# Moving a transformer block's later weight loads behind its first dense query copies, with a new prologue order

## The chip, the cores and the metric

One core of one Trainium2 chip. The metric is the device time of one execution in microseconds (us); lower is better. Times are medians of several runs, and runs of one kernel spread by 1 to 4 us, so differences of 1 us are read from repeated rounds or from the traces only.

## The reference, cut to what matters

```python
# x: 2048 tokens x 640; 32 query heads of 20, one key head, one value head; hidden size 1728; bf16
xn = layernorm(x)                                  # no scale, no shift
q, k, v = xn @ wq, xn @ wk, xn @ wv                # k and v are shared by all heads
p = softmax(q @ k.T / sqrt(20))                    # 32 heads x 2048 x 2048 scores
out = x + (p @ v) @ wo + silu(xn @ w1) @ w2
```

## The kernel before: the parts that matter here

The kernel is not written down instruction by instruction. A list scheduler with a small time model decides, while the program is built, which instruction each engine gets next; constants at the top of the file steer it. A changed constant or dependency can so reorder all engines. Where the model sees TensorE idle, the scheduler also gives it *filler products* with zeros, which add nothing to a result and are meant to keep its clock up; they count as busy in every view below.

The attention is done in *groups* of three (head, 512 queries) units, 43 groups in all, each in 16 *steps*, one for each tile of 128 keys: 688 steps. A step is three score products on TensorE (PE), and an exponential on ScalarE (ACT). Mostly ScalarE takes two of the three units (a tile 1024 wide) and VectorE (DVE) turns the third into an exponential by a clamp on integers; GpSimd (POOL) prepares what follows the clamp. In some steps ScalarE takes all three (1536 wide). The rule:

```python
    def want_dve(self, t):                     # may VectorE take the third unit of step t?
        if t < DVE_FROM or t % KT >= KT - NOD or t >= self.T - DVE_LAST:
            return False
        ...                                    # cut: how far VectorE's work reaches beyond TensorE's
        return back < DVE_TH
```

At the end of a group its result leaves PSUM through VectorE, is transposed by a DMA issued from SyncE's queue (SP), taken up by GpSimd, and its reciprocal is made on VectorE:

```python
        op = sc.dma("sp", lambda q: q.dma_start_transpose(self.UT[...], self.U[...]), [("U", up)], [("UT", up)], ...)
        ...                                    # four small GpSimd instructions
        sc.new("dve", 0.22, lambda v: v.reciprocal(rl, w[:, :, :, DH]), ...)
```

SyncE also issues nearly all loads, in order. In the kernel before, both fills of the query buffer, w1 and wo are given to it early, and w2 once the copy out of one of the last transposes is scheduled:

```python
        for par in range(2):
            ...                                # fill qT[:, :, par, :] with its constant rows
        load_w("sp", "1", ...)                 # w1, 5 pieces, 2160 KB
        load_w("sp", "o", ...)                 # wo, 5 pieces, 800 KB
...
                if n == max(i for i in range(13) if i not in DT):
                    load_w2()                  # w2, 14 pieces, 2160 KB
```

A *dense query tile* is a product with 128 rows of wq at once; its rows belong to several heads, so 7 small DMA copies carry it to its places before the scores of those heads can start. The *Newton steps* of the prediction are small instructions that make the reciprocal square roots of the normalization, for a batch of tiles of 128 tokens at once.

## Time and profile before

| kernel before | us |
|---|---|
| median of 3 runs (lowest, highest) | 739.36 (739.25, 740.0) |
| span of the profiled run | 738.2 |
| start of exponential 35, of exponential 40 | 70.3, 75.2 |
| from exponential 40 to the last, number 688 | 636.8 |
| from the start of the last exponential to the end (the tail) | 26.2 |

The table cuts the run where different things set the time. The start to exponential 40 is the prologue: loads, normalization, first products. The middle is the loop of exponentials. In the tail ScalarE has next to nothing to do, and TensorE works off what is left of the output products. The starts of single exponentials were counted in the trace.

Two more views than the prediction shows are needed. The first is VectorE's timeline at the eviction of group 0 (start, length, engine, line, operation):

```profile
53.95 0.68 DVE L972 CAST sbt<-psall 128x512 bf16<-128x512 f32 x1
```

The result was in SBUF at 54.6 us, so of the wait that the prediction calls hole C only 2 us were spent before the transpose's issue at 56.68, and 5.3 us after it. The second is TensorE's busy time, granted clock, DMA share and GB/s in stretches around that hole:

```profile
62.00:66.00 4.00, 1.22 (x21) 0.95 0.06 15
66.00:70.00 4.00, 3.67 (x25) 0.63 0.00 0
```

In the second stretch the clock is 0.63 of full speed: one stretch of 3.4 us, from 65.6 us, just as TensorE took up work again after its own idle time, was run at half clock.

### The profile page before, as it was taken

The numbers are of one execution on the slowest core, as the hardware profiler recorded it, in microseconds if no ns is written. First come the engines' busy times: TensorE is split into PE (matmuls) and PEld (weight loads), VectorE is DVE, ScalarE is ACT, GpSimd is POOL, SyncE is SP. The second block draws the span as 40 slices with busy tenths as digits, with TensorE's granted clock in tenths as the row PEclk, the third lists the DMA queues.
The fourth block names the chain that finished last, engine by engine and source line by source line (L and its number), as shares of the span: only waits on it lengthen the run. The fifth ranks groups of instructions, "written<-read, shape, count | busy, mean of one in ns | idle before, by whom it ended". The sixth has DMA issues, their size and how long they took to land.

```text
span 738.2 us, 18883 instructions
## 1 busy us (share of the span) xinstructions
PE 707.6 (96%) x6798; PEld 229.7 (31%) x6852; DVE 665.5 (90%) x1206; ACT 691.0 (94%) x780; POOL 538.4 (73%) x929
## 2 busy tenths in 40 slices
PE   9788999999999999999999999999999999999998
PEld 4422222233333223223333222222233332322235
DVE  7786998999999999989999999999999999989973
ACT  6886999999999999999999999999999999999940
POOL 5467777787787877777878877787788877777750
PEclk9999999999999999999999999999999999999999
DMA  6494010000003021100001101110002000200101
GB/s 191 80 338 108 20 25 17 21 17 16 9 16 44 17 58 40 32 10 9 9 8 27 33 16 40 54 32 16 8 9 44 10 8 16 80 9 8 31 16 36
DMA packets 58466, 29.14 MB, mean 39 GB/s; under 512 B 44390, under 2 KB 57734, under 8 KB 58374
## 3 DMA queue, kind: packets, MB, share of 16 engines
q1 hardware_dynamic: 56918, 27.71, 14.7%
q8 instruction: 56, 0.92, 0.5%
q10 hardware_dynamic: 1456, 0.22, 0.2%
q14 instruction: 36, 0.29, 0.1%
HBM read 11.36 MB, written 2.62 MB: 19 GB/s over the span
## 4 chain that ended last, share of the span: by engine, by line
PE 62%; ACT 17%; DVE 6%; issue 5%; POOL 1%; DMA 1%; DVEq 0%; ACTq 0%; POOLq 0%
PE psall L857 21%; PE psall L769 20%; ACT sbt L787 15%; PE psall L1146 9%; PE psall L1084 6%; DVE sbt L801 3%; PE psall L1151 2%; PE psall L1050 2%; ACT sbt L1092 1%; DVE sbt L869 1%; DMA sbt<-sbt 1%; DVE sbt L972 1%; PE psall L693 1%; POOL sbt L807 0%; DVE sbt L1057 0%
## 5 line engine op out<-in xcount | busy, mean ns | idle before, releaser
L787 ACT ACTIVATE sbt<-psall 128x1024 bf16<-128x1024 f32 (+2 forms) x688 | 657.8, 1091 | 16.8 <-PE psall L769 15.9
L807 POOL TENSOR_TENSOR sbt<-sbt 128x256 int32<-128x256 int32 x646 | 447.2, 698 | 149.3 <-DVE sbt L801 122.7
L801 DVE TENSOR_SCALAR sbt<-psall 128x512 int16<-128x512 f32 x646 | 432.5, 683 | 34.4 <-PE psall L769 26.4
L769 PE MATMUL psall<-sbt 32*128 32x512 bf16 x2048 | 269.1, 385 | 9.7 <-ACT sbt L787 4.7
L857 PE MATMUL psall<-sbt 128*32 128x512 bf16 x3524 | 270.2, 385 | 4.2 <-DVE sbt L869 2.0
L769 PEld LDWEIGHTS psall<-sbt 32*128 32x128 bf16 x2048 | 68.7, 91 | 252.8 <-issue 105.1
L869 DVE TENSOR_SCALAR sbt<-sbt 128x1536 int16<-128x1536 int16 (+2 forms) x230 | 134.8, 587 | 2.8
L857 PEld LDWEIGHTS psall<-sbt 128*32 128x32 bf16 x3524 | 67.8, 94 | 115.0 <-issue 75.4
L1146 PE MATMUL psall<-sbt 128*128 128x320 bf16 x448 | 86.2, 302 | 0.0
L1084 PE MATMUL psall<-sbt 128*128 128x512 bf16 (+1 forms) x242 | 75.7, 385 | 5.1 <-issue 3.7
L1146 PEld LDWEIGHTS psall<-sbt 128*128 128x128 bf16 x448 | 35.1, 97 | 43.4 <-issue 33.8
L1097 DVE SCALAR_TENSOR_TENSOR sbt<-sbt,psall 128x512 bf16<-128x512 bf16 (+1 forms) x56 | 38.1, 680 | 4.2 <-ACT sbt L1092 3.5
L1092 ACT ACTIVATE sbt<-psall 128x512 bf16<-128x512 f32 (+1 forms) x56 | 37.7, 674 | 0.0
L1084 PEld LDWEIGHTS psall<-sbt 128*128 128x128 bf16 (+1 forms) x280 | 18.8, 98 | 39.9 <-issue 29.6
L972 DVE CAST sbt<-psall 128x512 bf16<-128x512 f32 x43 | 29.3, 681 | 2.0 <-PE psall L857 1.9
L1151 PE MATMUL psall<-sbt 128*128 128x320 bf16 x144 | 28.7, 303 | 0.4 <-DVE sbt L1181 0.4
L1050 PE MATMUL psall<-sbt 128*128 128x512 bf16 (+1 forms) x81 | 26.6, 385 | 2.4 <-issue 1.4
L958 POOL TENSOR_TENSOR sbt<-sbt 128x240 bf16<-128x240 f32 (+2 forms) x44 | 25.7, 583 | 0.9 <-DMA sbt<-sbt 0.5
L944 POOL TENSOR_TENSOR sbt<-sbt 128x44 f32<-128x44 f32 x84 | 25.0, 298 | 1.0
L706 PE MATMUL psall<-sbt 128*128 128x512 bf16 (+2 forms) x67 | 17.5, 407 | 4.8 <-DVE sbt L1565 3.3
L942 POOL CAST sbt<-sbt 128x168 f32<-128x168 bf16 x42 | 14.2, 337 | 9.7 <-DMA sbt<-sbt 9.1
L1178 ACT ACTIVATE sbt<-psall 128x320 bf16<-128x320 f32 x4 | 1.5, 437 | 20.7 <-PE psall L1151 20.7
(94 smaller groups left out, 219.8 us busy)
## 6 DMA issues: line engine op xcount, KB each, us to landing
sbt<-in_A_x_dram SPq DMA_DIRECT2D x32, 160.0 KB, 3.6
out_dram<-sbt SPq DMA_DIRECT2D x15, 160.0 KB, 1.9
sbt<-in_B_w_dram SPq DMA_DIRECT2D x5, 432.0 KB, 7.4
sbt<-sbt SPq DMA_DIRECT2D x105, 20.0 KB
sbt<-in_B_w_dram SPq DMA_DIRECT2D x13, 160.0 KB, 5.8
sbt<-sbt SPq DMA_TRANSPOSE x68, 2.4
sbt<-sbt SPq DMA_DIRECT2D x1, 1024.0 KB, 7.3
sbt<-in_A_wo_dram SPq DMA_DIRECT2D x5, 160.0 KB, 6.8
```

What stands on the lines that cost most here:

```text
L769: ins = pe.matmul(self.bk(par3 + j), self.kT[r:r + SLOT, kk, kt * P:(kt + 1) * P], self.qT[r:r + SLOT, h // 4, (x // H) % 2, :], start=Tru ...
L787: return a.activation(self.E[:, b0 * QW:(b0 + na) * QW], self.ps[:, par3 * BANK:(par3 + na) * BANK], AF.Exp, scale=ACT_SCALE)
L801: return v.tensor_scalar(self.Z[:, zs, zp * QW:(zp + 1) * QW], self.bk(bb), 0.0, ZMAX, ALU.max, ALU.min)
L807: sc.new("pool", Y_TIME, lambda v: v.tensor_tensor(self.Y[:, zs, 1, zp * QW:(zp + 1) * QW].bitcast(I32), self.Z[:, zs, zp * QW:(zp + 1) * ...
L857: return pe.matmul(self.bk(UBANK, 0, QW, q * SLOT, (q + 1) * SLOT), self.v[:, w, kt, :], x, start=start, stop=stop, tile_position=(0, q * ...
L869: sc.new("dve", Y_SLOW + t_dve_4x(w), lambda v, k=k: v.tensor_scalar(self.Y[:, zs, k, 0:n * QW], Z, float(PH[k + 1][0]), None, ALU.add), z ...
L1050: return pe.matmul(self.bk(b, 0, QW, 0, rows), self.wq[:, k, lo:hi], self.xnT[:, k, c * QW:(c + 1) * QW], start=(k == 0), stop=(k == DC - 1))
L1084: return pe.matmul(self.bk(b, 0, QW, 0, rows), self.w1[:, k, fk * P:fk * P + rows], self.xnT[:, k, c * QW:(c + 1) * QW], start=(k == 0), s ...
L1092: sc.new("act", t_act(QW), lambda a: a.activation(t, src, AF.Tanh, scale=0.5), [("B", b)], [("tb", tp)], prio=X_PRIO, name=f"th{c}_{fk}")
L1097: sc.new("dve", t_dve_ps(QW), lambda v: v.scalar_tensor_tensor(out=self.hT[0:rows, fk, :], in0=t, scalar=1.0, in1=src, op0=ALU.add, op1=AL ...
L1146: return pe.matmul(self.bk(b, 0, 320), self.hT[0:rows, fk, i * P:(i + 1) * P], self.w2[0:rows, fk, e0:e0 + 320], start=(m == 0), stop=(m = ...
L1151: return pe.matmul(self.bk(b, 0, 320), self.oT[:, k, i * P:(i + 1) * P], self.wo[:, k, e0:e0 + 320], start=(m == 0 and src != "ps"), stop= ...
```

## The change

Its intent: give the first dense query tile's copies the queue before the bulk of w2, wo and the second fill, and search the prologue's order again with a scheduler that knows that GpSimd and VectorE hinder one another. Three settings of the loop go with it. The core of the diff:

```diff
+KT_ACT = (0,)                       # first step of each group: ScalarE takes all three units
-H_FIRST = 4
+H_FIRST = 8                         # hidden tiles ahead of the earlier chunk's output
-DVE_TH = 2.8
+DVE_TH = 3.4
-PV_HOLD = 9
+PV_HOLD = 11
-DT = (4, 5, 8, 9, 10, 11, 12, 13, 14, 15)
+DT = (4, 5, 6, 9, 10, 11, 12, 13, 14, 15)
-PRO = "t6 v0 k2 t7 k3 k4 q1 v1 v2 k5 k6 k7 v3 d0"
+PRO = "v0 t7 t8 v1 k2 k3 k4 q1 v2 d0 k5 k6 k7 v3"
-NW_ENG = ("dve", "pool", "dve", "pool")
+NW_ENG = ("dve", "dve", "dve")
-BATCHES = ((0, 4), (4, 8), (8, 12), (12, 16))
+BATCHES = ((0, 4), (4, 10), (10, 16))
 ... (cut: NORM_P, NORM_ENG, locks that keep VectorE and GpSimd apart in the model)
-        if t < DVE_FROM or ... or t >= self.T - DVE_LAST:
+        if t < DVE_FROM or ... or t >= self.T - DVE_LAST or t % KT in KT_ACT:
 ...
+            if c == 0 and m == 0:                       # first dense query tile: after its copies
+                self.late_loads(("qd", sl))
 ...
+        def late_loads(key):
+            load_w2([key])
+            load_w("sp", "o", ..., (), [key])           # wo
+            ...                                         # its scaling on GpSimd
+            qz(1, [key])                                # the second fill of the query buffer
```

More of the change, by code (lines that the diff above doesn't have):

```diff
@@ L75 @@
 UT_ISSUE = 1.05
-DT = (4, 5, 8, 9, 10, 11, 12, 13, 14, 15)
-NORM_P = 0.5
+DT = (4, 5, 6, 9, 10, 11, 12, 13, 14, 15)
+NORM_P = 4.5
 DVE_FROM = 8
-PRO = "t6 v0 k2 t7 k3 k4 q1 v1 v2 k5 k6 k7 v3 d0"
+PRO = "v0 t7 t8 v1 k2 k3 k4 q1 v2 d0 k5 k6 k7 v3"
 ACT_STATS = (4, 6, 9, 12, 14)
-NW_ENG = ("dve", "pool", "dve", "pool")
-NORM_ENG = ("pool", "pool", "pool", "pool", "dve", "act", "act", "dve", "act", "dve", "dve", "act")
-BATCHES = ((0, 4), (4, 8), (8, 12), (12, 16))
+NW_ENG = ("dve", "dve", "dve")
+NORM_ENG = ("pool", "pool", "pool", "pool", "act", "pool", "act", "act", "dve", "act", "act", "act")
+BATCHES = ((0, 4), (4, 10), (10, 16))
 class Op:
@@ L740, in want_dve @@
     def want_dve(self, t):
-        if t < DVE_FROM or t % KT >= KT - NOD or t >= self.T - DVE_LAST:
+        if t < DVE_FROM or t % KT >= KT - NOD or t >= self.T - DVE_LAST or t % KT in KT_ACT:
             return False
@@ L1302, in load_x, with load_w @@
             op.inc_no = 1
-        def load_w(eng, key, pieces, tag, nb, over=()):
-            deps = sc.deps_of((), [tag] + list(over))
+        def load_w(eng, key, pieces, tag, nb, over=(), extra=()):
+            deps = sc.deps_of(extra, [tag] + list(over))
             for f in pieces:
@@ L1327, in prologue, with load_w2 @@
                                                                self.B_w2[fk * P:fk * P + rows, :]))
-        def load_w2():
-            load_w("sp", "2", w2p, ("w2",), P * D * 2, [("xn", i) for i in range(14)] + [("idf",)])
+        def load_w2(extra):
+            load_w("sp", "2", w2p, ("w2",), P * D * 2, [("xn", i) for i in range(14)] + [("idf",)], extra)
         np_ = sc.new
@@ L1437, in norm @@
                 xa(n), self.xslot(n), self.rstd[:, n:n + 1], self.nb[:, n:n + 1], ALU.mult, ALU.add),
-                self.xkeys(n) + [("nb", n), ("rs", ra)], [("xn", n)], prio=prio, name=f"norm{n}")
+                self.xkeys(n) + [("nb", n), ("rs", ra)], [("xn", n)], prio=prio, name=f"norm{n}").lock = True
         def newton(a, b_, pr, eng):
@@ L1447, in nw @@
                 ch.append(np_(eng, 0.09 if eng == "dve" else 0.16, fn, r, w, prio=pr, name="nw"))
+                ch[-1].lock = True
                 if len(ch) > 1:
@@ L1496, in prologue, with qz @@
         tb = self.tb[:, 0, :]
-        for par in range(2):
+        def qz(par, extra=()):
             h0 = 2 if par == 0 else 0
             rep = bass.AP(self.tb, tb.offset, [list(tb.ap[0]), [0, HT - h0], list(tb.ap[1])])
-            op = sc.dma("sp", lambda q, par=par, h0=h0, rep=rep: q.dma_start(self.qT[:, h0:HT, par, :], rep), [("tb", 0)],
+            op = sc.dma("sp", lambda q: q.dma_start(self.qT[:, h0:HT, par, :], rep), [("tb", 0)] + list(extra),
                         [("qb", par, h) for h in range(4 * h0, H)], P * (HT - h0) * QW * 2, sem=sem(f"qz{par}"))
             op.inc_no = 1
+        qz(0)
         load_w("sp", "1", [lambda q, c=c: q.dma_start(self.w1[:, c, :], self.B_w1[c * P:(c + 1) * P, :])
                            for c in range(DC)], ("w1",), P * F * 2)
-        load_w("sp", "o", [lambda q, c=c: q.dma_start(self.wo[:, c, :], self.A_wo[c * P:(c + 1) * P, :])
-                           for c in range(DC)], ("wo",), P * D * 2)
+        def late_loads(key):
+            load_w2([key])
+            load_w("sp", "o", [lambda q, c=c: q.dma_start(self.wo[:, c, :], self.A_wo[c * P:(c + 1) * P, :])
+                               for c in range(DC)], ("wo",), P * D * 2, (), [key])
+            for c in range(DC):
+                pool(0.7, lambda g, c=c: g.tensor_scalar(self.wo[:, c, :], self.wo[:, c, :], 2.0, 1.0, ALU.mult, ALU.mult),
+                     [("wo",)], [("wo",)], prio=2.0)
+            qz(1, [key])
+        self.late_loads = late_loads
         def tr_job(n):
@@ L1523, in consume @@
                            prio=0.5 if n < 4 else 3.0, name=f"xT{n}")
-                if n == max(i for i in range(13) if i not in DT):
-                    load_w2()
             return Job(f"tr{n}", mms, xnk(n)[:1] + [("idb",)], consume)
@@ L1543, in consume @@
                                                                       ALU.mult), [("kT", j), ("offk",)],
-                       [("kT1", j)], prio=1.0, name=f"k1_{j}")
-                if j == KT // 2 - 1:
-                    for c in range(DC):
-                        pool(0.7, lambda g, c=c: g.tensor_scalar(self.wo[:, c, :], self.wo[:, c, :], 2.0, 1.0, ALU.mult,
-                                                                 ALU.mult), [("wo",)], [("wo",)], prio=2.0)
+                       [("kT1", j)], prio=1.0, name=f"k1_{j}").lock = True
             return Job(f"kv{j}", mms, [("xnT", 2 * j), ("xnT", 2 * j + 1), ("wk",), ("ost", 2, 0), ("ost", 2, 1)], consume)
```

## The prediction

> **What bounds the kernel now.** I read the page's busy shares first, then ACT's busy time in three stretches, then ACT's timeline through the prologue, then the other engines and the SP queue around its longest hole. Of the page, and of the stretches (busy us of ACT, clock, DMA share, GB/s):
>
> ```profile
> PE 707.6 (96%) x6798; PEld 229.7 (31%) x6852; DVE 665.5 (90%) x1206; ACT 691.0 (94%) x780; POOL 538.4 (73%) x929
> ...
> 20.00:80.00 60.00, 47.47 (x53) 0.94 0.58 166
> 80.00:700.00 620.00, 618.68 (x683) 1.00 0.10 24
> 700.00:738.20 38.20, 10.74 (x19) 1.00 0.10 27
> ```
>
> From 80 to 700 us ACT idles 1.3 us of 620: it works through the exponentials back to back, and nothing that only frees another engine can shorten this stretch. The 38 us at the end are other work (last products, output). Between 20 and 80 us ACT idles 60 - 47.5 = 12.5 us. A prologue change can win at most these, and pays for whatever it adds to ACT. ACT's timeline says where they are (start, length, count, idle before and its releaser):
>
> ```profile
> 23.13 1.73 ACT L1431 ACTIVATE sbt<-sbt 128x640 bf16<-128x640 bf16 x2 [0.99 <-DVE sbt L1468]
> ...
> 29.14 1.45 ACT L787 ACTIVATE sbt<-psall 128x1536 bf16<-128x1536 f32 x1 [2.53 <-PE psall L769]
> ...
> 40.55 1.94 ACT L787 ACTIVATE sbt<-psall 128x1024 bf16<-128x1024 f32 x2 [0.66 <-PE psall L769]
> 45.28 16.72 ACT L787 ACTIVATE sbt<-psall 128x1024 bf16<-128x1024 f32 x18 [2.80 <-PE psall L769]
> ...
> 67.94 1.94 ACT L787 ACTIVATE sbt<-psall 128x1024 bf16<-128x1024 f32 x2 [5.45 <-PE psall L769]
> ```
>
> Three holes: A (0.99 + 2.53 = 3.5 us) near 22 to 29 us, B (0.66 + 2.80 = 3.5 us) near 40 to 45, C (5.45 us) near 62.5 to 68; together 12.4.
>
> Hole A begins on VectorE, where nine tiny Newton steps on 128x4 values run beside GpSimd's four normalizations (18.38 to 21.84 us):
>
> ```profile
> 20.18 0.81 DVE L1457 TENSOR_TENSOR sbt<-sbt 128x4 f32<-128x4 f32 x1
> 21.03 0.82 DVE L1459 SCALAR_TENSOR_TENSOR sbt<-sbt 128x4 f32<-128x4 f32 x1
> ...
> 22.34 0.16 DVE L1457 TENSOR_TENSOR sbt<-sbt 128x4 f32<-128x4 f32 x1
> 22.54 0.16 DVE L1459 SCALAR_TENSOR_TENSOR sbt<-sbt 128x4 f32<-128x4 f32 x1
> ```
>
> The same step takes 0.82 us beside GpSimd and 0.16 us alone. Five slowed steps (0.53, 0.83, 0.81, 0.82, 0.42) cost 3.41 - 5 x 0.16 = 2.6 us. The copy out of the transpose of tile 6 waits behind them, and TensorE, in order, behind that copy.
>
> Hole B: step 14 needs the last key tile, whose product stands on TensorE behind 25 value products, after the last of ten transposes that SyncE issues from 19.29 to 37.4 us.
>
> Hole C starts in the SP queue (first two lines), shows on GpSimd (third) and then on VectorE (fourth):
>
> ```profile
> 49.09 7.55 SPq L1326 DMA_DIRECT2D sbt<-in_B_w_dram  x14
> 56.68 1.28 SPq L931 DMA_TRANSPOSE sbt<-sbt  x1
> ...
> 62.01 0.33 POOL L942 CAST sbt<-sbt 128x168 f32<-128x168 bf16 x1 [3.93 <-DMA sbt<-sbt]
> ...
> 64.27 0.23 DVE L949 RECIPROCAL sbt<-sbt 128x12 f32<-128x12 f32 x1 [3.73 <-POOL sbt L944]
> ```
>
> The transpose of group 0's result is issued at 56.68 behind the 14 loads of w2 and lands 5.3 us later; the median of the 42 such transposes is 2.4. GpSimd waits in order for it, VectorE for GpSimd, TensorE for VectorE, ACT for TensorE.
>
> **What the Trainium skill says.** "SBUF — State Buffer", the part on its two physically separate sides, says that VectorE in a two-port mode or with two SBUF inputs and GpSimd share one port pair as an exclusive lock: "the other fully blocks". The trace agrees: 0.82 against 0.16 us, and 0.82 is about one GpSimd normalization (0.88 us). "DMA: Bandwidth & Descriptors", Issuing engines are not separate DMA queues, says that all DMAs run on the same 16 engines and interleave; its Rules for kernel authors say to issue a DMA early and wait late. Hole C agrees: from 38 to 62 us the engines moved 334 GB/s at a DMA share of 1.02, and the small transpose waited. "Perfetto Trace Analysis", Identifying the Most-Contended Engine, takes occupancy as the measure for ScalarE but not matmul busy time for TensorE; so I follow ACT rather than PE's 96%.
>
> **The change part by part.** Counts come from the two instruction orders, durations from the rows of before.
>
> (1) The Newton batches become 4, 6 and 6 tiles, all on VectorE; 24 GpSimd steps of about 0.2 us go (4.8 us of an engine that is not the bound). The first six-tile batch comes ahead of GpSimd's normalizations, not beside them: most of the 2.6 us goes. That nothing overlaps is only the scheduler's model; no wait is added.
>
> (2) Six normalizations stand on ACT, against four. Two took 1.73 us, so + 2 x 0.87 = 1.7 us. Five stand in a row between exponentials 4 and 5, and need the statistics of all tiles. VectorE's order up to there, by its own rows: first batch from about 16.5 to 18.4 us; evictions and statistics 5.8 us, to 24.2; a copy 0.5; second batch 1.9, to about 26.5. Then 5 x 0.87 = 4.35 brings exponential 5 to about 30.9 us. Before, it came at 29.14, but with two more normalizations (1.7) still ahead of number 6: level, within an estimated 1 us. So hole A is filled with the moved work rather than won.
>
> (3) The last transpose should be issued about 35 us instead of 37.4, and the last key product stands ahead of step 11, before any value product. Hole B should nearly go: about -3 us.
>
> (4) Later loads: the queue becomes w1, four x tiles, three pieces of w2, the seven copies of the first dense q tile, eleven pieces of w2, wo, the 1024 KB fill of q, and only then the first result transpose (with two more behind it). What stands ahead of it is what stood before: w1 2160 + wo 800 + x 640 + w2 2160 + fills 1792 = 7552 KB, plus 128 KB of q copies. At the 334 GB/s of 38 to 62 us this is about 23 us, and the 5.4 us of copies may leave a gap of 1 or 2 us. From 35 us plus 2 to start, the transpose lands about 61 to 63 us; before it was 62.0. So I don't expect this part to relieve hole C by bandwidth. But the order is gentler: before, VectorE held the reciprocal behind its 23rd clamp (that of exponential 31), now behind its 24th (exponential 34, since the 33rd has none), and ACT arrives 3 us earlier. The chain from landing to the reciprocal was 62.01 to 64.27; from 62.6 it ends at about 65, and a clamp, a score and about 0.7 us later exponential 36 or 37 starts at about 66.4, where before number 33 started at 67.94: a gain of 1.5 + 3.5 x 0.93 = 4.8 us to this point, which holds (2), (3) and (4) together. If the transpose were in time, number 33 would start at about 59.5 (number 15 at 42.4, then 18 at 0.93 and one wide one): a gain of 8.4.
>
> (5) The first step of every group stays wholly on ACT (KT_ACT). Exponentials: 1536 wide 41 to 49, 1024 wide 632 to 625, 512 wide 15 to 14. By the busy time of the rows, 60.8/41 = 1.48, 597.4/632 = 0.945, 8.8/15 = 0.59: + 8 x 1.48 - 7 x 0.945 - 0.59 = + 4.7 us; where ACT runs back to back its starts are nearer 0.9 and 1.33 apart, so + 3.9. As ACT is the bound from 80 to 700 us, this lies on the path; about 0.9 of it falls before step 35, so + 3.0 to 3.8 remain. VectorE sheds 9 clamps of 0.67 us and about 5 us of their followers, about 11 us, which ACT's 1.3 us of idle cannot reward.
>
> (6) Eight h products before the earlier chunk's output: the same work, with one tanh (0.5 us) left for later. After the last scores 92 output products stand instead of 89: 3 x 0.13 = + 0.4 us.
>
> Sum: -4.8 + 3.4 + 0.5 + 0.4 = -0.5 if hole C stays in part; -8.4 + 4.3 = -4.1 if it goes.
>
> **Rivals.** *The late transpose remains the wait* (ahead: the same bytes in the same queue; against: it starts 2 us earlier, and consumers have more slack): 739.4 - 0.5, about 739. *The transpose comes in time*: -4.1, about 735; all holes gone, -12.4 + 4.7 + 1.7 + 0.4 = -5.6, about 734. *VectorE was the hidden pacer of the steady part* (90% busy; DVE releases many short TensorE waits), so its 11 us ease some of ACT's stretched exponentials: rows average 0.945 against 0.90 back to back, and if a tenth of that 632 x 0.04 = 25 us went, -2.5 more: about 731. *New conflict*: the second six-tile batch meets a GpSimd normalization, or five normalizations in a row starve the scores: +2 to +3, about 742.
>
> **Range and chances.** The change looks tuned for a gain, and my replay of orders is weakest in hole C, so I put the time between the first two rivals, nearer the second: 736.0 us, eight times in ten within 731 to 741. A gain over 2% is 14.8 us, more than all idle time of the prologue: 0.02. A loss over 2% would need a new stall of 15 us: 0.01. Within 2%: 0.97.
>
> **What would show it.** Right if: ACT's idle time between 20 and 80 us falls from 12.5 to some 4 to 6 us; no Newton step on VectorE takes 0.8 us; the 2.80 us wait near 45 us is gone; ACT stays 99% busy from 80 to 700 us; 49 wide exponentials are there. Hole C: the first result transpose lands at 61 to 63 us and GpSimd's wait for it stays above 3 us; if it lands before 59 us my queue argument is wrong and the time is nearer 733. If ACT shows idle time in the steady part, or the tail moves by over 1 us, the sum is wrong elsewhere.

## The result and the profile after

The changed kernel took 741.26 us (median of 4 runs, 741.11 to 744.0), the kernel before 739.31 on the same chip. The ratio is 1.0033, with a 95% interval of 1.0009 to 1.0057: the same at the 2% threshold, but slower, and 0.26 us above the predicted range of 731 to 741. Run again in a later batch the change gave 741.93 and 1.0026 (1.0012 to 1.0040): a small loss, not a gain.

The page's busy shares and ScalarE's stretches (busy us, clock, DMA share, GB/s) of the changed kernel:

```profile
PE 715.2 (97%) x6853; PEld 228.7 (31%) x6853; DVE 653.2 (88%) x1191; ACT 695.7 (94%) x782; POOL 526.4 (71%) x897
```

```profile
20.00:80.00 60.00, 50.74 (x54) 0.91 0.56 164
80.00:700.00 620.00, 619.17 (x683) 1.00 0.10 23
```

ScalarE's idle time in the prologue fell only from 12.5 to 9.3 us, and the middle is as full as before. The clock of the prologue fell from 0.94 to 0.91. (PE's 707.6 before against 715.2 is not 7.6 us more work: before, 54 matmul records are missing from the trace, 6798 against 6852 weight loads.)

ScalarE's timeline shows where the holes went (start, length, count, and in brackets the idle time before):

```profile
25.49 4.16 ACT L1434 ACTIVATE sbt<-sbt 128x640 bf16<-128x640 bf16 x5 [0.49 <-DVE sbt L1472]
29.56 7.26 ACT L788 ACTIVATE sbt<-psall 128x1536 bf16<-128x1536 f32 x6
37.08 1.02 ACT L788 ACTIVATE sbt<-psall 128x1024 bf16<-128x1024 f32 x1 [0.26 <-PE psall L770]
38.54 18.04 ACT L788 ACTIVATE sbt<-psall 128x1024 bf16<-128x1024 f32 x19 [0.44 <-PE psall L858]
...
68.32 1.94 ACT L788 ACTIVATE sbt<-psall 128x1024 bf16<-128x1024 f32 x2 [6.73 <-PE psall L770]
70.54 1.02 ACT L788 ACTIVATE sbt<-psall 128x1024 bf16<-128x1024 f32 x1 [0.29 <-PE psall L770]
71.99 1.02 ACT L788 ACTIVATE sbt<-psall 128x1024 bf16<-128x1024 f32 x1 [0.42 <-PE psall L770]
```

Holes A and B are gone: 0.49, 0.26 and 0.44 us stand where 3.5 and 3.5 stood. Hole C has grown from 5.45 to 6.73 us, and small waits follow it. Now the queue (SP), and the four engines that hand the wait on:

```profile
42.69 5.37 SPq L1067 DMA_DIRECT2D sbt<-sbt  x7
48.10 5.66 SPq L1329 DMA_DIRECT2D sbt<-in_B_w_dram  x11
53.80 2.48 SPq L1514 DMA_DIRECT2D sbt<-in_A_wo_dram  x5
56.32 0.69 SPq L1505 DMA_DIRECT2D sbt<-sbt  x1
57.06 12.59 SPq L932 DMA_TRANSPOSE sbt<-sbt  x2
```

```profile
48.66 0.68 DVE L973 CAST sbt<-psall 128x512 bf16<-128x512 f32 x1
63.79 0.33 POOL L943 CAST sbt<-sbt 128x168 f32<-128x168 bf16 x1 [7.56 <-DMA sbt<-sbt]
66.04 0.23 DVE L950 RECIPROCAL sbt<-sbt 128x12 f32<-128x12 f32 x1 [6.23 <-POOL sbt L945]
66.62 1.04 PE L858 MATMUL psall<-sbt 128*32 128x512 bf16 x8 [6.40 <-POOL sbt L808]
```

Group 0's result is in SBUF at 49.3 us, 5.3 us earlier than before. Its transpose stands in SyncE's queue for 7.7 us behind eleven pieces of w2, five of wo and a fill, is issued at 57.06, and GpSimd can take it only 6.7 us later, at 63.79; before, that was at 62.01. What the faster prologue won was spent in this queue, and 1.8 us more.

TensorE's busy time and clock after the hole:

```profile
62.00:66.00 4.00, 0.00 (x0) 0.60 0.28 22
66.00:70.00 4.00, 3.38 (x22) 0.50 0.09 22
70.00:74.00 4.00, 4.00 (x31) 0.62 0.05 11
```

TensorE was idle for 6.4 us (60.2 to 66.6) and then ran at half clock: the stretch lasts 10.2 us, from 62.8 to 73.0 us, three times the 3.4 us of before. Exponentials 36 to 40 start over 5.3 us, where the kernel before took 4.0. The Trainium skill, "TensorE: Matmul & The Clock Gate", Part 1: The HAM clock gate, says that an idle window of about 3.4 us halves TensorE's clock, that a busy window restores it, and that the window runs freely. The trace agrees on the length: the half-clock stretches last 3.4 and 10.2 us. It does not show a wholly idle window: in the 3.4 us before the fall at 62.8 us TensorE was busy for 0.8 us.

The account between the two profiled runs, by the cuts of the table:

| | before | after | difference |
|---|---|---|---|
| start of exponential 35 | 70.3 | 60.5 | -9.8 |
| exponential 35 to 40 | 4.9 | 13.1 | +8.2 |
| exponential 40 to 688 | 636.8 | 639.0 | +2.1 |
| tail | 26.2 | 26.9 | +0.8 |
| span | 738.2 | 739.5 | +1.3 |

Of the 9.8 us, 5.45 are hole C, which before lay ahead of number 33 and now lies ahead of number 36. Without it the prologue is 4.4 us faster. Hole C and the slow restart then take 8.2 instead of 5.45, and the loop and its tail take 2.9.

### The profile page after: what moved, and what is told of

It reads as the page before. It is cut to its first block, busy times and chain, and to the rows that moved or that the text cites. A ratio compares the mean times of both kernels' runs of the same rounds, so it can differ in the third digit from the quotient of the medians. Undisturbed runs are those within 1.5% of the kernel's fastest.

```text
span 739.5 us, 18880 instructions
## 1 busy us (share of the span) xinstructions
PE 715.2 (97%) x6853; PEld 228.7 (31%) x6853; DVE 653.2 (88%) x1191; ACT 695.7 (94%) x782; POOL 526.4 (71%) x897
## 4 chain that ended last, share of the span: by engine, by line
PE 71%; ACT 10%; DVE 5%; issue 4%; POOL 0%; DVEq 0%; ACTq 0%; POOLq 0%
PE psall L858 25%; PE psall L770 23%; PE psall L1149 10%; ACT sbt L788 8%; PE psall L1087 8%; DVE sbt L802 3%; PE psall L1051 2%; PE psall L1154 2%; ACT sbt L1095 2%; DVE sbt L1100 1%; DVE sbt L870 1%; PE psall L694 1%; DVE sbt L973 0%; PE psall L1217 0%; DVE sbt L1184 0%
## 5 line engine op out<-in xcount | busy, mean ns | idle before, releaser
L808 POOL TENSOR_TENSOR sbt<-sbt 128x256 int32<-128x256 int32 x637 | 438.9, 694 | 160.2 <-DVE sbt L802 140.3
L802 DVE TENSOR_SCALAR sbt<-psall 128x512 int16<-128x512 f32 x637 | 426.2, 685 | 47.6 <-PE psall L770 43.6
L770 PEld LDWEIGHTS psall<-sbt 32*128 32x128 bf16 x2048 | 69.1, 91 | 253.1 <-issue 76.5
L870 DVE TENSOR_SCALAR sbt<-sbt 128x1536 int16<-128x1536 int16 (+1 forms) x218 | 129.5, 596 | 2.2
L1087 PE MATMUL psall<-sbt 128*128 128x512 bf16 (+1 forms) x280 | 85.3, 384 | 2.8 <-DVE sbt L1100 2.6
L1149 PE MATMUL psall<-sbt 128*128 128x320 bf16 x448 | 84.0, 302 | 0.0
L1051 PE MATMUL psall<-sbt 128*128 128x512 bf16 (+1 forms) x95 | 28.7, 385 | 0.7 <-DVE sbt L1100 0.7
L1154 PE MATMUL psall<-sbt 128*128 128x320 bf16 x144 | 28.5, 303 | 0.3 <-DVE sbt L1184 0.3
L707 PE MATMUL psall<-sbt 128*128 128x512 bf16 (+1 forms) x74 | 18.7, 402 | 2.0 <-POOL sbt L1344 1.5
```

The costliest lines, as they stand in the source:

```text
L770: ins = pe.matmul(self.bk(par3 + j), self.kT[r:r + SLOT, kk, kt * P:(kt + 1) * P], self.qT[r:r + SLOT, h // 4, (x // H) % 2, :], start=Tru ...
L802: return v.tensor_scalar(self.Z[:, zs, zp * QW:(zp + 1) * QW], self.bk(bb), 0.0, ZMAX, ALU.max, ALU.min)
L808: sc.new("pool", Y_TIME, lambda v: v.tensor_tensor(self.Y[:, zs, 1, zp * QW:(zp + 1) * QW].bitcast(I32), self.Z[:, zs, zp * QW:(zp + 1) * ...
L870: sc.new("dve", Y_SLOW + t_dve_4x(w), lambda v, k=k: v.tensor_scalar(self.Y[:, zs, k, 0:n * QW], Z, float(PH[k + 1][0]), None, ALU.add), z ...
L1051: return pe.matmul(self.bk(b, 0, QW, 0, rows), self.wq[:, k, lo:hi], self.xnT[:, k, c * QW:(c + 1) * QW], start=(k == 0), stop=(k == DC - 1))
L1087: return pe.matmul(self.bk(b, 0, QW, 0, rows), self.w1[:, k, fk * P:fk * P + rows], self.xnT[:, k, c * QW:(c + 1) * QW], start=(k == 0), s ...
```

## The experiments

The theory: (i) the place of the first result transposes in SyncE's queue decides what the prologue's gain is worth; (ii) the hole costs more than its length, because TensorE restarts at half clock; (iii) the settings of the loop cost about 3 us. Rivals: the result transpose is not what the group waits for; moved work is only paid back later; the loop's settings pay for themselves. In what follows, e35 and e40 are the starts of exponentials 35 and 40; all from each run's one profile.

| run | median us | ratio to before (95%) | e35 | e40 | e40 to 688 | tail | span |
|---|---|---|---|---|---|---|---|
| before | 739.9 | 1 | 70.3 | 75.2 | 636.8 | 26.2 | 738.2 |
| the change (first profile) | 741.3 | 1.0033 (1.0009, 1.0057) | 60.5 | 73.6 | 639.0 | 26.9 | 739.5 |
| after_again | 741.9 | 1.0026 (1.0012, 1.0040) | 61.0 | 74.6 | 638.8 | 26.9 | 740.3 |
| tr_first | 736.0 | 0.9957 (0.9940, 0.9975) | 61.5 | 66.2 | 641.2 | 26.9 | 734.3 |
| split_late_2 | 735.7 | 0.9945 (0.9927, 0.9964) | 60.3 | 64.9 | 640.5 | 26.9 | 732.4 |
| before_w2_late | 737.3 | 0.9965 (0.9950, 0.9979) | 68.0 | 72.6 | 637.0 | 26.2 | 735.8 |
| loads_back | 747.3 | 1.0100 (1.0081, 1.0119) | 82.8 | 87.4 | 640.2 | 18.0 | 745.5 |
| steady_after | 741.9 | 1.0021 (1.0004, 1.0038) | 71.1 | 76.5 | 640.5 | 22.8 | 739.9 |
| steady_before | 747.2 | 1.0088 (1.0072, 1.0104) | 61.3 | 73.6 | 636.6 | 35.5 | 745.7 |

(The median of before is that of the later batches, 739.9 to 740.0; its profile is the first one. Each figure is rounded by itself, so a row's sum can be 0.1 off its span. The other runs' figures stand in their sections.)

### tr_first: the first result transpose ahead of the late loads

```diff
+            if g == 0:                                  # in end_group, after the transpose is given
+                self.late_loads(("U", 0))
-            if c == 0 and m == 0:                       # in the dense query tile
-                self.late_loads(("qd", sl))
```

> The changed kernel, with w2, wo and the second q fill queued only behind the first result transpose instead of ahead of it. My theory (the late transpose is the whole of hole C, with the half TensorE clock that follows it): the transpose lands within 3 us of its issue (6.7 before), GpSimd's wait for it falls from 7.6 to under 1.5 us, ACT's idle time between 20 and 80 us from 9.2 to about 2 us, the clock stays at 1.00 there, and the time falls by 7 to 9 us, to about 733. Rival (the loss is the work moved onto ACT): the hole goes but another in-order wait takes its place, time 739 or more.

Correct; 735.97 us, 0.9957 of the kernel before. Its queue, GpSimd's two pick-ups, and ScalarE's one new wait:

```profile
50.39 1.24 SPq L932 DMA_TRANSPOSE sbt<-sbt  x1
...
63.04 2.19 SPq L932 DMA_TRANSPOSE sbt<-sbt  x1
```

```profile
54.50 0.32 POOL L943 CAST sbt<-sbt 128x168 f32<-128x168 bf16 x1
...
68.73 0.32 POOL L943 CAST sbt<-sbt 128x168 f32<-128x168 bf16 x1 [1.92 <-DMA sbt<-sbt]
```

```profile
76.87 2.37 ACT L788 ACTIVATE sbt<-psall 128x1536 bf16<-128x1536 f32 x2 [1.82 <-PE psall L770]
```

The transpose was issued as soon as the result was in SBUF (49.69 + 0.68), hole C vanished, no half clock showed before the end, and e40 came 7.4 us earlier than in the changed kernel. The second transpose was issued 0.3 us after its result (62.06 + 0.68 us), but behind the moved loads it was picked up only 5.7 us later, and ScalarE's wait of 1.8 us followed. Theory (i) holds: this one place is worth 5 to 6 us of the change's time, where 7 to 9 were expected. The loop after e40 was 2.2 us longer than in the change, so some of the gain is given back.

### fill_hole: keep TensorE's clock through the hole

```diff
+        # behind the scores of step 34: 26 products with zeros, into the open bank, adding nothing
+        for _ in range(26):
+            pe.matmul(self.bk(UBANK, 0, QW, 0, 32), self.zero[:, 0:32], self.zero[:, 0:QW], start=False, stop=False, ...)
```

> The changed kernel with 26 extra products of zero weights (about 5.5 us) set on TensorE just ahead of the value product that waits in hole C; results are not altered. They end before that wait ends, so only the clock can change. If the half clock after the hole costs time: granted clock 1.00 between 62 and 74 us, exponentials 37 to 40 without their waits of 0.3 to 0.6 us, time lower by about 2 us, 739.3. If the clock plays no part: the time stays at 741.3.

Correct; 742.77 us, ratio 1.0035 (1.0022 to 1.0048): no gain in the whole. TensorE's busy time and clock over the hole:

```profile
62.00:66.00 4.00, 4.00 (x21) 1.00 0.76 95
66.00:70.00 4.00, 3.29 (x27) 1.00 0.00 0
```

The clock stayed at 1.00. From the end of group 0's reciprocal to exponential 36 it took 1.4 us instead of 2.05, and exponentials 36 to 40 took 3.6 us (69.45 to 73.08) instead of 5.3. So the half clock's local price is 2.3 us, 0.6 before exponential 36 and 1.7 after it; this part of theory (ii) is shown. In the total it was not seen. In the profiled run exponential 1 started 1.0 us later than in the change's, a half-clock stretch fell at 34.1 us and another at 279.9, exponential 35 started at 62.5, 2.0 us late, before the edit can have acted, and the loop after e40 took 640.9 us, 1.9 more than in the change. The timed runs' mean clocks are 0.995 in two and 0.997 to 0.998 in four, against 0.991 to 0.993 in the change; yet these four took 740.8 to 743.0 us, where the change took 741.1 to 744.0. Why the total did not gain stays open.

### no_kt_act: the rule on the first step taken out alone

```diff
-KT_ACT = (0,)
+KT_ACT = ()
```

> The changed kernel without the rule that keeps each group's first step on ACT (KT_ACT empty). My theory (ACT paces the steady part, so the extra width is paid in full): wide exponentials fall from 49 to about 40, the time falls by 3 to 4 us, to about 737.5; hole C is as it was. Rival (the rule relieves VectorE at each group's start and pays for itself): 741 or more, with more ACT idle time after 80 us.

748.99 us, 1.0117 (1.0103 to 1.0132), and the result was wrong (relative error 0.408); why was not found, so only its times are used, and with care. Only 10 exponentials are 1536 wide, against 49, where about 40 were expected; with the threshold at 2.8, in steady_before below, 39 are; that threshold and H_FIRST are all that differs. VectorE's busy time rose to 684.9 us. ScalarE idled 9.0 us between 80 and 700 us (0.8 in the change), as the rival said. It reached its last exponential at 699.2 us, 13.5 us before the changed kernel's, and the end came 8.5 us later. TensorE's busy time in the tail, first of this run, then of the changed kernel:

```profile
699.20:748.10 48.90, 43.62 (x287) 1.00 0.19 52
```

```profile
712.60:739.50 26.90, 23.55 (x177) 0.98 0.08 26
```

TensorE is 97% busy in the changed kernel (93% without the 24.0 us in which only filler products ran). Work taken from ScalarE does not shorten the run when TensorE does not get through its own earlier; the difference comes back as output products after the last exponential. My expectation that the rule's price lies in full on the path fell in this form.

### h_first_4: four hidden tiles first

```diff
-H_FIRST = 8
+H_FIRST = 4
```

> The changed kernel with four h products before the earlier chunk's output, as before the change. My theory: this part is worth only the tail: 89 or 90 output products after the last scores instead of 92, time lower by 0 to 1 us. Rival (the job order matters in the steady part): a change of over 2 us either way, seen as ACT idle time between 80 and 700 us.

Correct; 743.40 us, 1.0056 (1.0040 to 1.0072). The tail was 28.0 us, not shorter than the 26.9 of the change: the setting is not what lengthened it. By the ratios the run took about 2 us longer than the change (the intervals overlap), where 0 to 1 less was expected. This expectation was wrong.

### split_late: the loads in two steps, first try

The late loads are split: w2 after the first result transpose; wo, its scaling and the second fill after the second.

```diff
+            if g < 2:                                   # in end_group; the call in the dense tile goes
+                self.late_loads(("U", g))
 ...
+            if key == ("U", 0):
+                load_w2([key])
+                return
             load_w("sp", "o", ...)                      # then the scaling and qz(1, [key])
```

> The changed kernel with its late loads in two steps: w2 is given to SyncE once the first result transpose is, wo with its scaling and the second fill of the query buffer only once the second result transpose is. In tr_first the first transpose was issued at 50.4 us and cost ScalarE nothing, but the second stood behind w2, wo and the fill and made a wait of 1.8 us at 76.9 us. Theory (the place of the transposes in SyncE's order is what the prologue's gain hangs on): that wait goes too, ScalarE is idle no more than 2 us between 20 and 80 us outside the first group, no half clock between 60 and 80 us, 734.0 us against 736.0 of tr_first. Rival (the second transpose waits for something else, such as its own group's end, or wo arriving later holds up the first output projection): the same 736, or a new wait later.

735.32 us, 0.9927, but the result was wrong (relative error 0.93). The one difference from the mended run below is that the fill comes later too, so that is where the fault came in; a likely reason, not tested, is that the tile which the fill copies had been used again by then. Its times are left out of the argument.

### split_late_2: the same, with the fill back where it was correct

```diff
-            if c == 0 and m == 0:
-                self.late_loads(("qd", sl))
+            if g < 2:                                   # in end_group
+                self.late_loads(("U", g))
 ...
+            if key == ("U", 0):
+                load_w2([key])
+                qz(1, [key])
+                return
             load_w("sp", "o", ...)                      # after the second transpose, with the scaling
```

> As split_late, mended: w2 and the second fill of the query buffer go to SyncE after the first result transpose (where tr_first has them and was correct), wo and its scaling after the second. Theory: correct, the second transpose is issued within 1 us of its group's eviction, ScalarE waits for no scores between 60 and 110 us, and the time is that of split_late, 734.5 to 735.5 us, so at or a little under the 736.0 of tr_first and 6 below the changed kernel. Rival (what was gained in split_late hung on the wrong data or on the fill's place): 736 or more.

Correct; 735.68 us, 0.9945 of the kernel before. Its queue at the two transposes:

```profile
49.16 1.29 SPq L932 DMA_TRANSPOSE sbt<-sbt  x1
...
61.51 1.21 SPq L932 DMA_TRANSPOSE sbt<-sbt  x1
```

Both are issued as their results come (the evictions ended at 49.13 and 61.48 us), and ScalarE's longest wait between 20 and 110 us is 0.5 us, after which 31 instructions follow without a gap:

```profile
38.43 29.38 ACT L788 ACTIVATE sbt<-psall 128x1024 bf16<-128x1024 f32 x31 [0.50 <-PE psall L858]
```

It is busy 58.88 us of the 60 between 20 and 80. The time is 0.2 us above the range that was expected. It is the fastest correct version found, and it beats both kernels. Against tr_first (0.9957) the intervals overlap, so the second step's own worth, 1.3 us at e40, is not shown in the total.

### before_tr_first and before_w2_late: the same idea in the kernel before

In before_tr_first, w2, wo and the second fill go behind the first result transpose in the kernel before.

```diff
-                if n == max(i for i in range(13) if i not in DT):
-                    load_w2()
 ...                                                    # wo and the second fill leave their early places too
+            if g == 0:                                  # in end_group
+                self.late_loads(("U", 0))
```

> The kernel before with one thing changed: w2, wo with its scaling and the second fill go behind the first result transpose, nothing else of the change. Theory (hole C is one hole of 5.45 us in the kernel before, owed to the transpose's place alone): about 734.5 us, 5 less than before, and the holes A and B stay as they were. Rival (the hole is set by the group's own work on TensorE and VectorE, or later work fills up what is won): within 2 us of before.

Correct; 759.18 us, 1.0251 (1.0230 to 1.0271), so the expectation was off by 25 us. The transpose was issued at 56.73 us and GpSimd did not wait for it; but in this kernel the dense query tile's copies come *after* that transpose. The moved loads took their place in the queue (w2 at 58.34, wo at 65.05, the fill at 68.28, the copies at 69.06 us), ScalarE waited 10.3 us in one piece, and e40 came at 89.6:

```profile
69.06 6.59 SPq L1068 DMA_DIRECT2D sbt<-sbt  x7
```

```profile
74.31 0.60 ACT L1094 ACTIVATE sbt<-psall 128x512 bf16<-128x512 f32 x1 [10.29 <-DMA sbt<-sbt]
```

So both the copies and the transposes have to stand ahead of the bulk loads. In before_w2_late, w2 alone is moved, behind the second transpose:

```diff
+            if g == 1:                                  # in end_group
+                self.late_w2(("U", 1))                  # w2's 14 pieces
-                if n == max(i for i in range(13) if i not in DT):
-                    load_w2()
```

> The kernel before with w2's fourteen loads alone moved behind the second result transpose, so that the first transpose and the copies of the dense query tile go first; wo and both fills stay. In the kernel before the first group's result left the bank at 54.6 us, the transpose was issued at 56.7 and GpSimd went on at 62.0. Theory (the loads cost the transpose 2 us of issue and about 1.5 us of landing): issued at 54.7, GpSimd at about 58, the hole of 5.45 us down to about 2, and 736 us, 3.5 less than before. Rival (before_tr_first's 759 shows that the kernel before does not bear its loads moved at all): 739.5 or more.

Correct; 737.34 us, 0.9965 (0.9950 to 0.9979), 2.5 us less than before, where 3.5 was expected. The transpose and GpSimd's pick-up:

```profile
56.47 1.23 SPq L931 DMA_TRANSPOSE sbt<-sbt  x1
```

```profile
59.81 0.32 POOL L942 CAST sbt<-sbt 128x168 f32<-128x168 bf16 x1
```

GpSimd took the result 3.3 us after issue, without a wait, where it was 5.3 us behind w2's loads, and the hole of 5.45 us became one of 1.54:

```profile
65.72 1.94 ACT L787 ACTIVATE sbt<-psall 128x1024 bf16<-128x1024 f32 x2 [1.54 <-PE psall L769]
```

The exponentials themselves began 1.5 us later in this run and the clock was halved at 48.2 us; e40 gained 2.6. Fourteen loads put in another place gained 2.5 us, where the whole change lost 1.9.

### loads_back: the changed kernel with its loads where they were

```diff
         qz(0)
+        qz(1)
 ...                                         # wo early, w2 at the copy out of the last transposes; no late_loads
```

> The changed kernel with its loads where the kernel before has them (both fills and wo early, w2 behind the transposes of the normalized rows), all else of the change stays. Theory (in the changed kernel the late loads keep the first transpose from 49.3 to 57.1 us on SyncE and then lengthen its landing to 6.7 us): the loads are issued some 5 us earlier, but the copies of the dense query tile wait behind w2, so what the transpose wins the scores lose: ScalarE's idle time of 9.3 us from 20 to 80 us stays between 7 and 13 us, and 741 us, within 2 of the changed kernel. Rival (the late loads are the whole of the loss): 737 or less.

Correct; 747.30 us, 1.0100 (1.0081 to 1.0119). I had expected the two orders to be level. Its queue:

```profile
47.13 7.70 SPq L1327 DMA_DIRECT2D sbt<-in_B_w_dram  x14
54.94 5.42 SPq L1067 DMA_DIRECT2D sbt<-sbt  x7
60.40 10.21 SPq L932 DMA_TRANSPOSE sbt<-sbt  x2
```

The copies went out 12.2 us later than in the changed kernel (54.94 against 42.69), the transpose 3.3 us later, ScalarE was idle for 20.9 us between 20 and 80 us, where 7 to 13 were expected, and e40 came 13.7 us later, at 87.4; the shorter tail gave 8.9 us of that back. So the move that gives the change its name is good by itself: under the new prologue it is worth 5.4 us of the time. It was put in the right place for the copies, and the wrong one for the transposes. This transpose, behind the small copies instead of bulk loads, was picked up 2.4 us after its issue (GpSimd at 62.80), against 6.7.

### steady_after and steady_before: the loop's settings alone

KT_ACT, DVE_TH and H_FIRST of the change put into the kernel before (steady_after), and those of before put into the change (steady_before, shown here; steady_after is the reverse).

```diff
-KT_ACT = (0,)
+KT_ACT = ()
-H_FIRST = 8
+H_FIRST = 4
-DVE_TH = 3.4
+DVE_TH = 2.8
```

> The kernel before with the three steady settings of the changed kernel alone: the rule on the first key tile, the threshold at 3.4, eight hidden tiles first; its prologue and its loads stay. Theory (these settings cost 2.9 us between exponential 40 and the end): 742 us, 2 to 3 more than before. Rival (they cost nothing by themselves, as a search that chose them would suggest): within 1 us of 739.5.

> The changed kernel with the three steady settings of the kernel before: no rule on the first key tile of a head, the VectorE threshold at 2.8 instead of 3.4, four hidden tiles first instead of eight; its prologue and its late loads stay. Theory (the change's prologue wins about 1.6 us up to exponential 40 and its steady settings lose about 2.9 from there to the end): 738 us, 2 to 3 less than the changed kernel, with the stretch from exponential 40 to the end near the 663.0 us of the kernel before. Rival (the loss comes from the order that the prologue leaves behind, not from the settings): 741, as the changed kernel.

Both correct. Steady_after: 741.91 us, 1.0021 (1.0004 to 1.0038): a loss of about 1.5 us, less than expected. The loop took 3.7 us longer and the tail 3.3 less. Steady_before: 747.18 us, 1.0088 (1.0072 to 1.0104), where 738 was expected: the loop fell back to 636.6 us as expected, but the tail rose to 35.5. So neither "these settings cost 2.9 us" nor "they are harmless" is right for both prologues. What ScalarE saves in the loop, TensorE returns in the tail, by an amount that depends on the order that the scheduler finds. Why it returned 8.5 us for 2.4 in steady_before is shown in part only. TensorE's idle time there, summed over its records, is 24.4 us, and 24.3 in the change. But the time in which it ran nothing but filler products is 27.3 us against 24.0 (131 such products against 114), and the time with other products 693.9 against 691.3. So over half of the 6.1 us between the two spans went into filler, which the order decides; no run without filler was made, and the rest stays open.

### after_again: the change beside the last three

> The changed kernel itself, beside the three of this batch on the same chip. All theories expect the ratio of 1.0033 against the kernel before again, within its interval (1.0009 to 1.0057), a half clock episode somewhere between 60 and 75 us, and ScalarE idle about 9 us between 20 and 80 us.

Correct; 741.93 us, 1.0026, as before. The half-clock stretch was there again (10.2 us, from 63.5), ScalarE was idle 9.8 us between 20 and 80 us, and the first result transpose was issued at 57.92 and picked up at 64.95 us.

## Why the prediction was wrong, by its own steps

**Bounds and holes: right, with one omission.** ScalarE is over 99% busy in the middle in both kernels, and the three holes were the whole of what the prologue could win; split_late_2 fills them. Omitted was TensorE, whose share the prediction set aside: it finishes last, and no_kt_act and steady_before show that less work on ScalarE is not less time. Of the signs that the prediction named, ScalarE's idle time from 20 to 80 us fell to 9.3 us, not to 4 to 6; GpSimd's wait stayed above 3 us (7.56), as it said.

**Parts (1) and (2), Newton steps and normalizations: right.** No Newton step on VectorE takes over 0.26 us. Two of them, where 0.82 us stood before:

```profile
24.09 0.17 DVE L1461 TENSOR_TENSOR sbt<-sbt 128x6 f32<-128x6 f32 x1
24.29 0.17 DVE L1463 SCALAR_TENSOR_TENSOR sbt<-sbt 128x6 f32<-128x6 f32 x1
```

Exponential 5 started at 29.56 us, where 30.9 was predicted. This is what the Trainium skill, "SBUF — State Buffer", in its part on the two physically separate sides, leads one to expect once the two engines' work no longer overlaps: GpSimd stood still from 23.10 to 27.23 us.

**Part (3), hole B: right.** The 2.80 us wait near 45 us is gone.

**Part (4), the late loads: the step that failed.** It put the landing at 61 to 63 us and exponential 36 at 66.4, "a gain of 4.8 us to this point". GpSimd took up the transpose at 63.79 and 64.95 us in the two profiles, and number 36 started at 68.3 and 69.5: 1.9 to 3.1 us later. The mechanism, that the same bytes ahead of the transpose would keep it late, was right. Of the terms of its sum two were too small and one was missing. The landing was worked out at the 334 GB/s of the kernel before; in both profiles of the change the engines moved 306 and 305 GB/s from 38 to 62 us, and the pick-up came 1.2 and 2.4 us after the 62.6 of the sum. From the end of the reciprocal to exponential 36 the sum has about 1.4 us; it took 2.05, and 1.4 in fill_hole, where the clock was not halved. And exponentials 36 to 40, for which the sum has no term, took 5.3 and 5.1 us, where the kernel before took 4.0 and fill_hole 3.6: after TensorE's idle 6.4 us the clock was at half for 10.2 us. So up to e40 the gain was 1.6 us in the one profile and 0.7 in the other, not 4.8.

**Part (5) and (6), the loop and the tail: sign right, size within 2 us.** Predicted were +3.4 to the loop, +0.5 for a tanh and +0.4 in the tail, +4.3 together; measured +2.1 and +0.8, +2.9 together. The 49 wide exponentials are there. That this is ScalarE's added work alone is refuted by steady_before.

**The headline: a choice that went against its own sum.** The sum with hole C staying was -0.5, about 739, and the prediction itself argued that the transpose would stay late. It then took 736, "nearer the second" rival, because the change "looks tuned". The measured difference is +1.9 us by medians. So of the 5.3 us by which 736.0 was missed, 2.8 are that choice and 2.5 are the sum's own: 3.2 us lost in part (4), 1.4 won back in parts (5) and (6), and the rest lies between the profiles and the medians. The runs do say what it would have taken: with the transposes in time, tr_first took 735.97 and split_late_2 735.68 us, where the second rival had said 735.

## What to carry to other kernels

When bulk loads are moved in an in-order queue, list what comes to stand behind them, and give the queue first whatever has a consumer waiting; here copies, then the small transposes, then the weights: 5 to 6 us for two lines of order. Price a stall of TensorE at its length plus a slow restart, here 2.3 us up to exponential 40, though the total of fill_hole did not show it. And where two engines are both over 90% busy, follow both to the end, with filler work counted apart: time taken off one may come back as the other's tail.

## What the Trainium skill lacked or had wrong

- "TensorE: Matmul & The Clock Gate", Part 1: The HAM clock gate, and its closing table under "Why this matters for your kernels", speak of an idle window and of gaps over about 3 us. In split_late_2 the clock halved with no such gap: TensorE was busy 1.99 us of the 3.4 us window ahead, its longest gap 1.01 us, and then ran 3.4 us at half clock. (The page does tell, further down in Part 1, of a kernel whose clock fell through frequent short gaps, but gives no busy share for it.) The stretches (busy us of TensorE, weight loads, VectorE, ScalarE, GpSimd; clock, DMA share, GB/s):

```profile
267.50:270.90 3.40, 1.99 (x18) 0.58 (x17) 3.27 (x7) 3.40 (x5) 2.72 (x5) 1.00 0.09 23
270.90:274.30 3.40, 3.40 (x17) 0.62 (x18) 2.50 (x6) 2.55 (x4) 1.50 (x3) 0.50 0.18 41
```

- The same page says that a busy window restores the clock, not how busy it must be. In the changed kernel a window 89% busy by the records did not (66.2 to 69.6 us, after an idle one) and the next, fully busy, did; in the kernel before one 83% busy, and another 69% busy (24.6 to 28.0 us), were followed by the full clock. The ends of matmuls are modelled in the trace, so which share decides is open.
- "DMA: Bandwidth & Descriptors", Issuing engines are not separate DMA queues, says that DMAs interleave on the same 16 engines; the page gives no figure for what a small one pays when it is issued behind large ones. Here the same transpose was picked up 2.4 us after issue behind copies of up to 20 KB (loads_back), 5.3 behind fourteen pieces of w2 (before), and 6.7 behind eleven pieces of w2, wo and a 1024 KB fill (the change).
- No page has the warning about the same queue: an instruction ready to be issued waits for the issue of all bulk loads ahead of it. It was 7.7 us here, for eleven pieces of w2, five of wo and one fill that took 8.8 us to issue.
